# A decode step on one core: K0 and V6 loaded in two parts, V7 in four, q and gate/up as loops over padded x, and the last output rows behind the block's barrier

## The chip, the cores and the metric

The kernel runs on one core of a Trainium2 chip. The metric is device time in microseconds, as the median over runs. A profiled execution gives the trace: busy time of each engine, waits, and DMA packets. PE is TensorE, DVE VectorE, ACT ScalarE, POOL GpSimd; SP issues the transfers.

## What is computed

One decode step of attention beside a small feed-forward block, mixed by a gate. x is one row of 512; the K and V caches hold 8 groups of 32768 rows of 128 numbers in bf16, that is 8 MB per group for K and as much for V. Four query heads share each group.

```python
x = A_x
g = sigmoid((x * gate_w).sum(-1))
q = (x @ wq)                      # 32 heads of 128
p = softmax(q @ k.T * 128 ** -0.5)
a = (p @ v).reshape(1, 4096) @ wo # wo: 4096 x 512
b = (silu(x @ w_gate) * (x @ w_up)) @ w_down   # 1792 wide
out = g * a + (1 - g) * b         # 512 numbers
```

## The kernel before

**Memory.** `page` holds three pages of 8 MB (64 KB per partition). Pages 0 and 1 take the K blocks in turn, page 2 the V blocks. At first page 2 holds wq and the gate and up weights; at the end page 0 holds w_down and wo.

**The order of the transfers** is SP's program (L330 to L359): wq, x and gate_w, gate, up, K0, K1, V0, K2, V1, K3, and so on. `load_k(j)` (L312) waits until DVE has transposed the block that used the page before (`sem_tr`); `load_v(j)` (L323) waits until PE has used the whole V block before (`sem_v_done`, raised after every 8 matmuls), V0 until PE has finished gate and up (`sem_pe_h`). K7 comes in two halves. After V6 come w_down (L342), the first piece of wo (`load_wo(0)`, two of 32 columns), the five parts of V7 (`V7_CUTS`, each as soon as the V6 rows in its place are used), and the other five pieces of wo (`WO_CUTS`). Last, SP waits for the result row and stores it (L358). All of it runs through SP's one queue, in this order.

**q, gate and up.** PE turns x into a column `xT` (L369), and multiplies it with wq in 32 matmuls (L384): the weights are one column of x, and the result goes to one of four strips of 32 PSUM partitions, so that four neighbouring matmuls use different strips of the array. DVE brings q into `qblk` and `qcur` (L609 to L629), with four small matmuls of PE between (L397). Then 32 matmuls do gate and up in the same manner (L409), and ACT and DVE make the hidden vector t (L538, L632 to L646).

**The groups.** For each group DVE transposes the K block in 64 units (L687); PE multiplies each unit with the group's query (`emit_s`, L431); DVE takes the maximum (L696), POOL spreads it over the partitions (L294), ACT exponentiates (L552) and rearranges the weights into `ET` (L565). PE multiplies them with V one group later (`emit_v`, 64 matmuls, L455), after the scores of the group behind; then ACT copies the sum, PE transposes it (`emit_reduce`) and DVE picks out the four heads (L675). PE and DVE run this as loops (`hinted`, L212) with a branch for each kind of turn and a hint that says early where the loop's last branch will go.

**The end.** PE multiplies t with w_down (`emit_wd`) while V7 lands. After V7 DVE makes the attention vector `O2` and PE multiplies it with wo piece by piece: the first 24 columns into `ps_w` (`emit_wide`, L500), which DVE copies to `part` (L733); the next four into `ps_c` by `emit_rows` (L230): two matmuls of 256 columns for each column of wo, the first with 32 weight columns of which only the last is not zero (`O2z`), the second with one, so that the two halves of the row come to lie on partitions 31 and 32. Then PE turns its loop once more, and in the `Else` branch (L525) `part` is summed over its four strips (`selz` as weights, fp32) and the last two pieces of wo are added. DVE casts two rows (L745) and SP stores them. The block ends with a barrier of all engines (L253): every engine drains and signals, POOL releases them. Behind it SP waits for the store.

Of the kernel before, what the change touches and what calls it, by code (L numbers as in the profile page):

```python
# [14 lines left out]
def bass_gated_mix__gqa_block_cached__swiglu_ffn__decode_kernel(  # L15
# [23 lines left out]
    KC = D // 128  # L39
# [19 lines left out]
    WO_CUTS = [0, 2, 16, 24, 28, 30, 32]  # L59
    KW = 3  # L60
    KL = 4
# [4 lines left out]
    OW = NOUT // RPS  # L66
# [15 lines left out]
    V7_CUTS = [0, 32, 96, 160, 224, 256]  # L82

    with ExitStack() as es:
# [7 lines left out]
        sem_k = [S_(f"s_k{i}") for i in range(K_PAGES)]  # L92
        sem_k7 = S_("s_k7")
        sem_v = S_("s_v")
# [17 lines left out]
        sem_pe_sum = S_("s_pe_sum")  # L112
        sem_dve_x = S_("s_dve_x")
# [35 lines left out]
        res_row = T("res_row", [64, OW], BF16)  # L149
# [21 lines left out]
        q_row = slot[:, 0 : 2 * RQ * DH]  # L171
        q_blk = slot[:, 2 * RQ * DH : 4 * RQ * DH]
        sg = acc[:, 0:FS]
        t_row = slot[:, 0:FS]
        t_blk = slot[:, D : D + FS]
# [54 lines left out]
        def emit_rows(pe, lhs, rhs, last):  # L230
            for e in range(RPS):
                ins = pe.matmul(  # L232
                    ps_c[32 * e : 32 * e + (1 if e else SW), 0:OW],
                    lhs(e),
                    rhs[:, e * OW : (e + 1) * OW],
                    start=False,
                    stop=last,
                    skip_group_check=True,
                )
            return ins  # L240

        def emit_wo(pe, k):
# [8 lines left out]
            return ins  # L251

        with nc.Block("main") as block:  # L253
# [50 lines left out]
            def _(sp):  # L304
# [8 lines left out]
                def load_k(j):  # L313
# [36 lines left out]
                load_wo(0)  # L350
# [7 lines left out]
                sp.dma_start(  # L358
                    out[0, 0, :].rearrange("(e c) -> e c", e=RPS), res_row[SW - 1 : SW + 1, :]  # L359
                ).then_inc(sem_out, 16)  # L360

            @block.tensor
            def _(pe):
                def emit_q():
# [12 lines left out]
                    pe.wait_ge(sem_dve_prod, 1)  # L377
                    pe.wait_ge(sem_q, 16)
                    pe.wait_ge(sem_psw, 1)
                    for c in range(KC):  # L380
                        for b in range(2):
                            for s in range(NSTRIP):
                                g = 2 * s + b
                                ins = pe.matmul(  # L384
                                    ps_sc[32 * s : 32 * s + 1, b * 512 : (b + 1) * 512],
                                    xT[:, c : c + 1],
                                    wq_v[:, c, g * 512 : (g + 1) * 512],
                                    start=(c == 0),
                                    stop=(c == KC - 1),
                                    skip_group_check=True,  # L390
                                )
                    ins.then_inc(sem_pe_q, 1)
# [12 lines left out]
                    for w, (sem, base) in enumerate(((sem_fg, S_G0), (sem_fu, S_U0))):  # L405
                        pe.wait_ge(sem, 16)
                        for c in range(KC):
                            for s in range(NSTRIP):
                                ins = pe.matmul(  # L409
                                    ps_sc[32 * s : 32 * s + 1, base : base + FS],  # L410
                                    xT[:, c : c + 1],
                                    wgu[:, w, c, s * FS : (s + 1) * FS],
                                    start=(c == 0),
                                    stop=(c == KC - 1),
                                    skip_group_check=True,
                                )
                    ins.then_inc(sem_pe_h, 1)
# [27 lines left out]
                def emit_v(p):  # L445
                    part_at = pe.compute_val(((p + 7) >> 4) * 16 + 1)
                    pe.wait_ge(sem_v, p * 16)
# [42 lines left out]
                def emit_wide():  # L490
# [19 lines left out]
                    emit_wo(pe, KW).then_inc(sem_late, 1)  # L510

                emit_q()
                with hinted(pe, "groups", 1, G + 4) as (p, arm):
# [11 lines left out]
                    with pe.Else():  # L525
                        pe.wait_ge(sem_dve_w, 1)
                        emit_rows(pe, lambda e: selz[:, SW - 1 : SW] if e else selz[:, :], part, False)
                        for k in range(KL, len(sem_wo)):
                            ins = emit_wo(pe, k)
                        ins.then_inc(sem_pe_sum, 1)  # L530

            @block.scalar
            def _(act):
# [3 lines left out]
                act.wait_ge(sem_pe_h, 1)  # L537
# [39 lines left out]
            def _(dve):  # L577
# [6 lines left out]

                dve.memset(ps_sc[:, :], 0.0).then_inc(sem_psw, 1)
# [4 lines left out]
                for sem in sem_v7[1:] + [sem_k7, sem_acc]:  # L590
# [7 lines left out]
                dve.tensor_copy(xT[:, :], xg[:, 0, :]).then_inc(sem_dve_x, 1)  # L598
                dve.wait_ge(sem_dve_x, 1)
# [7 lines left out]
                dve.wait_ge(sem_pe_q, 1)  # L607
# [168 lines left out]
```

## Time and profile before

| | |
|---|---|
| median of 3 runs | 351.38 us (351.13 to 351.65) |
| the profiled execution | 352.33 us, its span 350.8 us |
| busy: PE, DVE, ACT | 174.7, 190.8, 92.9 us |
| moved by DMA | 148.14 MB, 422 GB/s over the span |
| weight-load and matmul records on PE | 2723 and 2723 |

A line of a group names the source line, engine and operation, then output and inputs, the number of instructions and their time. "DMA to landing" is the time from a transfer's issue to the last of its sixteen signals, each from one DMA engine. Issue time plus this is the moment at which the block can be used. The chain of waits lists start, length and what ran. A timeline row has in brackets how long its engine was idle before, and what ended that.

### The profile page before, as it was taken

What the parts mean: (1) busy time and instruction counts of PE and PEld (TensorE: products, weight loads), DVE (VectorE), ACT (ScalarE), POOL (GpSimd) and SP (SyncE); (2) the same over time, 40 slices, a digit from 0 to 9 for tenths busy, and PEclk for the clock granted to TensorE, in tenths of its full rate; (3) what the DMA queues carried; (4) which work ended last, traced back from release to release, by engine and by line L of the source; (5) the groups of instructions that cost most, each with busy time, mean ns of one, the idle gap of its engine ahead of it and who ended that gap; (6) DMA issues with size and microseconds to landing.
All of it is one profiled execution on the core that took longest, in us unless ns stands there. A gap on an engine that the chain in (4) does not pass through costs nothing.

```text
span 350.8 us, 7554 instructions
## 1 busy us (share of the span) xinstructions
PE 174.7 (50%) x2723; PEld 106.3 (30%) x2723; DVE 190.8 (54%) x309; ACT 92.9 (26%) x220; POOL 8.3 (2%) x29
## 2 busy tenths in 40 slices
PE   0430155455745570556435571557145585547546
PEld 0110144344234420443124321443034334422112
DVE  3060299899169801995069802993089729930001
ACT  1020000470480057003530057003800056036100
POOL 4000000000000000000000000000000000010000
PEclk9999999999975567555655566555855565559955
DMA  8998998999989999999899899998998999989994
GB/s 336 412 508 359 478 478 359 478 433 404 478 359 463 441 411 456 396 463 456 381 471 456 389 456 419 441 456 381 471 456 389 407 430 478 456 349 420 430 420 169
DMA packets 4475, 148.14 MB, mean 422 GB/s; under 512 B 501, under 2 KB 505, under 8 KB 1017
## 3 DMA queue, kind: packets, MB, share of 16 engines
q1 hardware_dynamic: 4472, 148.12, 98.3%
q8 instruction: 1, 0.02, 0.0%
q14 instruction: 2, 0.01, 0.0%
HBM read 148.11 MB, written 0.00 MB: 422 GB/s over the span
## 4 chain that ended last, share of the span: by engine, by line
DMA 63%; PE 15%; DVE 14%; issue 7%; SPq 1%; DVEq 0%
DMA page<-in_A_k_cache_dram 48%; DVE slot L687 13%; DMA page<-in_A_v_cache_dram 8%; DMA page<-in_A_wo_dram 7%; PE ps_sc L431 7%; PE ps_o L455 7%; PE ps_c L232 1%; SPq L306 0%; SPq L348 0%; SPq L334 0%; DVE oT L675 0%; DVEq L683 0%; DVE res_row L745 0%; DVEq L666 0%; SPq L330 0%
## 5 line engine op out<-in xcount | busy, mean ns | idle before, releaser
L687 DVE STREAM_TRANSPOSE slot<-page 128x512 f32<-128x512 f32 x256 | 167.0, 690 | 101.0 <-DMA page<-in_A_k_cache_dram 89.3
L431 PE MATMUL ps_sc<-qcur,slot 128*128 128x16 bf16 x2048 | 103.5, 179 | 126.9 <-DVE slot L687 113.4
L431 PEld LDWEIGHTS ps_sc<-qcur,slot 128*128 128x128 bf16 x2048 | 80.9, 107 | 151.0 <-issue 150.1
L455 PE MATMUL ps_o<-page,ET 128*16 128x512 bf16 x512 | 46.8, 541 | 21.0 <-issue 12.3
L565 ACT ACTIVATE ET<-E 32x256 bf16<-32x256 bf16 x128 | 52.8, 412 | 1.4
L547 ACT ACTIVATE nbias<-gmax 128x4 f32<-128x4 f32 x8 | 1.6, 206 | 185.7 <-POOL gmax L294 185.7
L455 PEld LDWEIGHTS ps_o<-page,ET 128*16 128x16 bf16 x512 | 16.1, 117 | 48.2 <-issue 34.5
L552 ACT ACTIVATE E<-ps_sc,nbias 128x256 bf16 x32 | 21.8, 851 | 1.7 <-ACT nbias L547 1.7
L696 DVE TENSOR_REDUCE pmax<-ps_sc 128x4 f32<-128x1024 f32 x8 | 9.8, 1225 | 4.7 <-PE ps_sc L431 4.7
L719 DVE TENSOR_REDUCE oT<-ps_o 128x4 f32<-128x64 f32 x1 | 0.2, 224 | 20.5 <-PE ps_o L469 20.5
L561 ACT ACTIVATE acc<-ps_o 128x512 f32<-128x512 f32 x8 | 4.8, 606 | 22.0 <-PE ps_o L455 22.0
L547 ACT ACT_TABLE_LOAD x8 | 10.3, 1283 | 0.1
L294 POOL PARTITION_ALL_REDUCE gmax<-pmax x8 | 3.0, 372 | 293.5 <-DVE pmax L696 293.5
L552 ACT ACTIVATION_READ_ACCUMULATOR E<-ps_sc,nbias x32 | 9.2, 287 | 0.0
L469 PE MATMUL ps_o<-ident_f,acc 128*128 128x128 f32 x32 | 5.7, 305 | 5.6 <-ACT acc L561 4.9
L369 PE MATMUL ps_m<-eye,E 2*128 2x2 bf16 x4 | 0.3, 164 | 13.3 <-DMA E<-in_gate_w_dram 13.3
L469 PEld LDWEIGHTS ps_o<-ident_f,acc 128*128 128x128 f32 x32 | 3.6, 150 | 10.1 <-ACT acc L561 8.4
L481 PE MATMUL ps_w<-page,vec 128*1 x14 | 5.3, 376 | 2.2 <-issue 0.9
L711 DVE TENSOR_REDUCE oT<-ps_o 128x4 f32<-128x64 f32 x1 | 0.2, 224 | 8.9 <-PE ps_o L469 8.9
L598 DVE CAST xT<-ps_m 128x4 bf16<-128x4 f32 x1 | 0.2, 163 | 8.9 <-PE ps_m L369 8.9
L369 PEld LDWEIGHTS ps_m<-eye,E 2*128 2x128 bf16 x4 | 0.2, 108 | 13.2 <-issue 13.2
L574 ACT ACTIVATE acc<-ps_o 128x512 f32<-128x512 f32 x1 | 0.6, 597 | 13.4 <-PE ps_o L455 13.4
(63 smaller groups left out, 44.7 us busy)
## 6 DMA issues: line engine op xcount, KB each, us to landing
page<-in_A_k_cache_dram SPq DMA_DIRECT2D x2, 4096.0 KB, 41.8
page<-in_A_v_cache_dram SPq DMA_DIRECT2D x3, 2048.0 KB, 13.5
page<-in_A_wq_dram SPq DMA_DIRECT2D x1, 4096.0 KB, 12.3
page<-in_A_v_cache_dram SPq DMA_DIRECT2D x2, 1024.0 KB, 13.0
page<-in_B_w_gate_dram SPq DMA_DIRECT2D x1, 1792.0 KB, 15.5
page<-in_B_w_up_dram SPq DMA_DIRECT2D x1, 1792.0 KB, 19.3
page<-in_B_w_down_dram SPq DMA_DIRECT2D x1, 1792.0 KB, 30.7
page<-in_A_wo_dram SPq DMA_DIRECT2D x1, 1792.0 KB, 23.5
```

Of the source, the lines that this page charges most:

```text
L232: ins = pe.matmul(ps_c[32 * e : 32 * e + (1 if e else SW), 0:OW], lhs(e), rhs[:, e * OW : (e + 1) * OW], start=False, stop=last, skip_grou ...
L294: pool.partition_all_reduce(gmax[:, :], pmax[:, :], 128, ReduceOp.max).then_inc(sem_gmax, 1)
L431: ins = pe.matmul(ps_sc[:, bass.ds(c0 + u * (SLOTS * RPU * NS) + (s * RPU + r) * NS, NS),], sv[:, s, r, e // 2, e % 2, :], qcur[:, e, :], ...
L455: ins = pe.matmul(ps_o[32 * c : 32 * c + VW, :], ET[:, k * VW : (k + 1) * VW], rows(V_PAGE, n, n + RQ), start=(k < NSTRIP), stop=(k >= NT ...
L469: ins = pe.transpose(ps_o[:, q * 128 : (q + 1) * 128], acc[:, q * 128 : (q + 1) * 128], ident_f[:, :],)
L481: pe.matmul(ps_w[0:1, :], vec[:, bass.ds(n, 1)], page[:, bass.ds(n * NOUT + o0, NOUT)], start=False, stop=False, skip_group_check=True,)
L547: act.activation(nbias[:, :], gmax[:, :], ACT.Copy, scale=-SCALE).then_inc(sem_nbias, 1)
L552: act.activation(ev[:, h, :, :], scv[:, h, :, :], ACT.Exp, bias=nbias[:, h : h + 1], scale=SCALE, accum_out=esum[:, bass.ds(j * HPG + h, 1 ...
L561: act.activation(acc[:, :], ps_o[:, :], ACT.Copy).then_inc(sem_acc, 1)
L565: ins = act.activation(etv[QP * i : QP * (i + 1), :, g, :], E[QP * g : QP * (g + 1), i * w : (i + 1) * w].rearrange("p (f m) -> p f m", f=KH),
L687: dve.transpose(slot_f[:, s * (SLOT // 2) : (s + 1) * (SLOT // 2)].rearrange("p (x g b) -> p g x b", g=NQ, b=QP), kp[:, f, :, tu * UW : (t ...
L696: dve.tensor_reduce(pmax[:, :], ps_sc[:, p * RB * NS : (p + 1) * RB * NS].rearrange("p (x h) -> p h x", h=HPG), AX.X, ALU.max,).then_inc(s ...
```

## The change

- K0 is loaded in two halves, like K7; DVE waits for the second (`sem_k0`) in the middle of the group.
- V6 is loaded in two parts, rows 0 to 160 and 160 to 256 (`V6_CUT`, `sem_v6`); V7 in four instead of five, the first with 128 of the 256 rows. All seven pieces of wo follow V7; before there were six, the first ahead of V7.
- q and gate/up become two loops of four turns with eight matmuls each. The weights are 128 columns out of `xz`, which is zero but for x in one column, shifted so that the result falls on the strip wanted. The other strips get zero added; so all matmuls accumulate onto the zeroed `ps_sc`. DVE zeroes `xz` (in `slot`) first and copies x into it; `q_row` and `t_row` move to `E`. Gate and up now stand ahead of the small matmuls for q, and `sem_pe_q` and `sem_pe_h` count the turns.
- `emit_rows` uses four strips with 128 output columns each instead of two with 256. `part` is added inside `emit_wide`, between the first and the second piece of wo that go to `ps_c`.
- The last two pieces of wo, the cast (now 128 x 128) and the store stand behind the block's barrier; the store is split between SP's and ACT's queues.

```diff
-    WO_CUTS = [0, 2, 16, 24, 28, 30, 32]
+    WO_CUTS = [0, 8, 16, 20, 24, 28, 30, 32]
-    KL = 4
+    KL = 5
+    OC = NOUT // 128
+    XW = 96 + 128
-    V7_CUTS = [0, 32, 96, 160, 224, 256]
+    V7_CUTS = [0, 128, 192, 224, 256]
+    V6_CUT = 160
...
-            for e in range(RPS):
+            for oc in range(OC):
+                e = oc % RPS
                 ins = pe.matmul(
-                    ps_c[32 * e : 32 * e + (1 if e else SW), 0:OW],
+                    ps_c[32 * oc : 32 * oc + (1 if e else SW), 0:128],
                     lhs(e),
-                    rhs[:, e * OW : (e + 1) * OW],
+                    rhs[:, oc * 128 : (oc + 1) * 128],
...
+        def store(eng, k):
+            n = RPS * 128
+            eng.dma_start(
+                out[0, 0, n * k : n * (k + 1)].rearrange("(c n) -> c n", c=RPS),
+                res_row[64 * k + SW - 1 : 64 * k + SW + 1, :],
+            ).then_inc(sem_out, 16)
...
-                    if j < G - 1:
+                    late = {0: sem_k0, G - 1: sem_k7}.get(j)
+                    if late is None:
                         cache(A_k_cache, j, p).then_inc(sem_k[p], 16)
                     else:
                         cache(A_k_cache, j, p, 0, NT // KH).then_inc(sem_k[p], 16)
-                        cache(A_k_cache, j, p, NT // KH, NT).then_inc(sem_k7, 16)
+                        cache(A_k_cache, j, p, NT // KH, NT).then_inc(late, 16)
...
-                        sp.wait_ge(sem_pe_h, 1)
-                    cache(A_v_cache, j, V_PAGE).then_inc(sem_v, 16)
+                        sp.wait_ge(sem_pe_h, KC)
+                    if j < G - 2:
+                        cache(A_v_cache, j, V_PAGE).then_inc(sem_v, 16)
+                    else:
+                        cache(A_v_cache, j, V_PAGE, 0, V6_CUT).then_inc(sem_v, 16)
+                        cache(A_v_cache, j, V_PAGE, V6_CUT, NT).then_inc(sem_v6, 16)
...
-                load_wo(0)
                 for k, sem in enumerate(sem_v7):
                     a, b = V7_CUTS[k], V7_CUTS[k + 1]
                     sp.wait_ge(sem_v_done, VTURN * (G - 1) + b // (RQ * VB))
                     cache(A_v_cache, G - 1, V_PAGE, a, b).then_inc(sem, 16)
-                for k in range(1, len(sem_wo)):
+                for k in range(len(sem_wo)):
                     load_wo(k)
-                sp.wait_ge(sem_dve_row, 1)
-                sp.dma_start(
-                    out[0, 0, :].rearrange("(e c) -> e c", e=RPS), res_row[SW - 1 : SW + 1, :]
-                ).then_inc(sem_out, 16)
...
+                    def strips(c, base, n, width, at, ps):
+                        x = [pe.compute_val(c * XW + (96 - 32 * s)) for s in range(NSTRIP)]
+                        w = [pe.compute_val(c * n + (base + at(i))) for i in range(2 * NSTRIP)]
+                        for i in range(2 * NSTRIP):
+                            ins = pe.matmul(
+                                ps_sc[:, ps(i) * 512 : ps(i) * 512 + width],
+                                slot[:, bass.ds(x[i % NSTRIP], 128)],
+                                page[:, bass.ds(w[i], width)],
+                                start=False,
+                                stop=False,
+                                skip_group_check=True,
+                            )
+                        return ins
+
+                    with pe.Fori(0, KC, 1) as c:
+                        strips(
+                            c, w0, H * DH, 512, lambda i: (2 * (i % 4) + i // 4) * 512, lambda i: i // 4
+                        ).then_inc(sem_pe_q, 1)
+                    pe.wait_ge(sem_fg, 16)
+                    pe.wait_ge(sem_fu, 16)
+                    with pe.Fori(0, KC, 1) as c:
+                        strips(
+                            c, w1, F, FS, lambda i: (i // 4) * KC * F + (i % 4) * FS, lambda i: 2 + i // 4
+                        ).then_inc(sem_pe_h, 1)
...
+                        if n == V6_CUT:
+                            pe.wait_ge(sem_v6, late_at)
...
-                    emit_wo(pe, KW).then_inc(sem_late, 1)
+                    emit_wo(pe, KW)
+                    pe.wait_ge(sem_dve_w, 1)
+                    emit_rows(pe, lambda e: selz[:, SW - 1 : SW] if e else selz[:, :], part, False).then_inc(
+                        sem_late, 1
+                    )
+                    for k in range(KW + 1, KL):
+                        emit_wo(pe, k)
...
-                    with pe.Else():
-                        pe.wait_ge(sem_dve_w, 1)
-                        emit_rows(pe, lambda e: selz[:, SW - 1 : SW] if e else selz[:, :], part, False)
-                        for k in range(KL, len(sem_wo)):
-                            ins = emit_wo(pe, k)
-                        ins.then_inc(sem_pe_sum, 1)
...
+                dve.memset(slot[:, 0 : KC * XW], 0.0).then_inc(sem_xz, 1)
...
+                dve.wait_ge(sem_xz, 1)
+                dve.tensor_copy(xz[:, :, 96], xg[:, 0, :]).then_inc(sem_xz, 1)
...
                             if t == KHU:
+                                if p == 0:
+                                    dve.wait_ge(sem_k0, 16)
...
-                    with dve.Else():
-                        dve.wait_ge(sem_pe_sum, 1)
-                        dve.tensor_copy(res_row[:, :], ps_c[0:64, 0:OW]).then_inc(sem_dve_row, 1)
-
-        nc.sync.wait_ge(sem_out, 16)
+
+        pe, dve = nc.tensor, nc.vector
+        for k in range(KL, len(sem_wo)):
+            ins = emit_wo(pe, k)
+        ins.then_inc(sem_pe_sum, 1)
+        dve.wait_ge(sem_pe_sum, 1)
+        dve.tensor_copy(res_row[:, :], ps_c[:, 0:128]).then_inc(sem_dve_row, 1)
+        for k, eng in enumerate((nc.sync, nc.scalar)):
+            eng.wait_ge(sem_dve_row, 1)
+            store(eng, k)
+        nc.sync.wait_ge(sem_out, 32)
```

More of the change, by code (lines that the diff above doesn't have):

```diff
@@ L92, in bass_gated_mix__gqa_block_cached__swiglu_ffn__decode_kernel @@
         sem_k = [S_(f"s_k{i}") for i in range(K_PAGES)]
+        sem_k0 = S_("s_k0b")
         sem_k7 = S_("s_k7")
+        sem_v6 = S_("s_v6")
         sem_v = S_("s_v")
@@ L148, in bass_gated_mix__gqa_block_cached__swiglu_ffn__decode_kernel @@
         selz = T("selz", [128, SW], FP32)
-        res_row = T("res_row", [64, OW], BF16)
+        res_row = T("res_row", [128, 128], BF16)
         eye2 = T("eye2", [2, 2], BF16)
@@ L170, in bass_gated_mix__gqa_block_cached__swiglu_ffn__decode_kernel @@
         x2 = E[0:2, 0:D]
-        q_row = slot[:, 0 : 2 * RQ * DH]
+        xz = slot[:, 0 : KC * XW].rearrange("p (c m) -> p c m", c=KC)
+        q_row = E[:, 0 : 2 * RQ * DH]
         q_blk = slot[:, 2 * RQ * DH : 4 * RQ * DH]
         sg = acc[:, 0:FS]
-        t_row = slot[:, 0:FS]
-        t_blk = slot[:, D : D + FS]
+        t_row = E[:, 0:FS]
+        t_blk = E[:, D : D + FS]
         spread = ET[:, 0 : NSTRIP * 128].rearrange("p (s m) -> p s m", s=NSTRIP)
@@ L377, in emit_q @@
                     pe.wait_ge(sem_dve_prod, 1)
+                    pe.wait_ge(sem_xz, 2)
                     pe.wait_ge(sem_q, 16)
                     pe.wait_ge(sem_psw, 1)
[L380 to L392, printed above, removed]
+                    def strips(c, base, n, width, at, ps):
[21 more added lines that the diff above has]
+                        ).then_inc(sem_pe_h, 1)
                     pe.wait_ge(sem_const, 4)
@@ L404, in emit_q @@
                     ins.then_inc(sem_pe_qp, 1)
[L405 to L417, printed above, removed]
                 sv = slot[:, :].rearrange(
@@ L589, in _ @@
                 dve.sem_inc(sem_sc, SLOTS)
-                for sem in sem_v7[1:] + [sem_k7, sem_acc]:
+                for sem in sem_v7[1:] + [sem_v6, sem_k7, sem_acc]:
                     dve.sem_inc(sem, 1)
@@ L606, in _ @@
                 )
-                dve.wait_ge(sem_pe_q, 1)
+                dve.wait_ge(sem_pe_q, KC)
                 dchain(
```

6 lines of the change are left out of this document (4 added, 2 removed).

## The prediction

> **What bounds the kernel now.** I read the page first: the span, the DMA queue, the chain by engine.
>
> ```profile
> span 350.8 us, 7554 instructions
> ...
> q1 hardware_dynamic: 4472, 148.12, 98.3%
> ...
> DMA 63%; PE 15%; DVE 14%; issue 7%; SPq 1%; DVEq 0%
> ```
>
> The kernel moves 148 MB through one queue whose packets fill 98.3% of the span, 344.8 us. The engines matter in two ways only: by when they let SP issue the next transfer, and by what they do after the last byte. So next comes the chain of waits, and with it each issue with its time to landing, in the view by source line:
>
> ```profile
> 63.35 35.62 DMA page<-in_A_k_cache_dram
> ...
> 319.62 26.26 DMA page<-in_A_wo_dram
> ```
>
> ```profile
> L306 SPq DMA_DIRECT2D page<-in_A_v_cache_dram x1: 328/328/328, 95.7 to 95.7; - x1
> DMA to landing us min/median/max: 23.6/23.6/23.6
> ...
> L306 SPq DMA_DIRECT2D page<-in_A_k_cache_dram x1: 432/432/432, 96.1 to 96.1; - x1
> DMA to landing us min/median/max: 42.6/42.6/42.6
> ...
> L306 SPq DMA_DIRECT2D page<-in_A_v_cache_dram x1: 328/328/328, 129.7 to 129.7; - x1
> DMA to landing us min/median/max: 28.3/28.3/28.3
> ```
>
> K2, the third K block, lands at 63.35 + 35.62 = 98.97; V1 at 119.3, K3 at 138.7, V2 at 158.0. Blocks of 8 MB follow each other by 19.3 to 19.4; V1 alone needs 20.4. It was issued at 95.7, only 3.2 us before K2's landing, and **1.0 us is lost**. V2, issued 9.0 us ahead of K3's landing, loses nothing. So on the last DMA engine V1's stream begins 98.97 + 1.0 - 95.7 = 4.3 us after its issue (counted in landing times). The second place with little in hand is V7:
>
> ```profile
> L342 SPq DMA_DIRECT2D page<-in_B_w_down_dram x1: 432/432/432, 286.5 to 286.5; - x1
> DMA to landing us min/median/max: 30.7/30.7/30.7
> ...
> L348 SPq DMA_DIRECT2D page<-in_A_wo_dram x1: 432/432/432, 287.0 to 287.0; - x1
> DMA to landing us min/median/max: 30.9/30.9/30.9
> ...
> L306 SPq DMA_DIRECT2D page<-in_A_v_cache_dram x1: 328/328/328, 314.1 to 314.1; - x1
> DMA to landing us min/median/max: 6.4/6.4/6.4
> ...
> L348 SPq DMA_DIRECT2D page<-in_A_wo_dram x2: 432/432/432, 320.1 to 320.6; - x2
> DMA to landing us min/median/max: 26.4/26.5/26.6
> ```
>
> w_down lands at 317.2, the first piece of wo at 317.9, the first 1 MB of V7 (issued at 314.1) at 320.5. A megabyte takes 19.35/8 = 2.4, so 0.2 is lost here and the stream began about 4.0 after the issue. The last piece of wo lands at 320.6 + 26.6 = 347.2. From there to the end is a tail of **3.6 us**:
>
> ```profile
> 345.72 0.69 DVE L733 COPY acc<-ps_w 128x512 f32<-128x512 f32 x1 [3.63 <-PE ps_w L500]
> ...
> 346.18 0.42 PE L232 MATMUL ps_c<-page,slot 128*32 128x256 bf16 x1
> ...
> 347.20 1.06 PE L232 MATMUL ps_c<-acc,selz 128*32 128x256 f32 x4 [0.17 <-issue]
> ...
> 349.16 0.42 DVE L745 CAST res_row<-ps_c 64x256 bf16<-64x256 f32 x1 [2.75 <-PE ps_c L232]
> 349.61 0.27 SPq L358 DMA_DIRECT2D out_dram<-res_row  x1
> ```
>
> The fp32 row of `part` begins at 347.20, when all of wo has landed: it stands behind a turn of the loop. The last two pieces of wo follow it, then a cast and the store, which takes 350.8 - 349.61 = 1.2.
>
> **The change part by part.** The sum is made against the profiled execution (span 350.8, own time 352.33). That lies 0.95 above the median of 351.38; I take the difference from the one and put it on the other.
>
> *K0 in halves, with the q and gate/up loops ahead of it.* What the first transposes waited for, and what now comes late:
>
> ```profile
> L306 SPq DMA_DIRECT2D page<-in_A_k_cache_dram x2: 452/474/495, 2.8 to 3.3; - x2
> DMA to landing us min/median/max: 38.1/47.6/57.0
> ```
>
> ```profile
> 13.55 0.16 DVE L598 CAST xT<-ps_m 128x4 bf16<-128x4 f32 x1 [8.92 <-PE ps_m L369]
> ...
> 13.96 3.58 PE L384 MATMUL ps_sc<-page,xT 128*1 128x512 bf16 x32 [0.45 <-DVE prod_col L600]
> ...
> 21.96 0.18 DVE L629 COPY qcur<-qblk 128x64 bf16<-128x64 bf16 x1
> ...
> 279.62 6.51 PE L455 MATMUL ps_o<-page,ET 128*16 128x512 bf16 x64 [1.81 <-issue]
> ...
> 309.36 1.23 DVE L696 TENSOR_REDUCE pmax<-ps_sc 128x4 f32<-128x1024 f32 x1 [0.58 <-PE ps_sc L431]
> ...
> 313.00 5.19 PE L455 MATMUL ps_o<-page,ET 128*16 128x512 bf16 x64 [3.68 <-DMA page<-in_A_v_cache_dram]
> ```
>
> K0 lands at 40.9, so its first half at 31.2; K1 at 60.3. Before, four strips of PE columns ran beside each other: 3.58/8 = 0.45 us per four. A padded x fills all 128 columns, so its matmuls run one after another. No row has such a one alone: from above 0.45 each, 14.4 us for 32; from below the pace at which V6 beats V5 (the colder V5 takes 6.51/64 each, V6 saves 1.3 in its last part, which comes to about 0.22 per four), 7.0. PE starts cold and is then busy without a break, so I take 9 for q and 6.5 for gate/up: done near 29.5. The small matmuls for q now stand behind gate/up, and of the 4.4 us from the end of q (17.5) to `qcur` (22.0) most follows: transposes begin near 33 to 34. A half group lasts 11 us, so K0's second half is there in time, and group 0 is done near 56, before K1 lands. In the trace group 0 ended at 63.35 and V1 was issued 32.4 later; from 60.3 the same 32.4 give 92.7 at the latest: 6.3 us in hand instead of 3.2, more than the 4.3 needed. **-1.0** on every later landing. The zeroing of 896 columns lies in DVE's idle 8.92 us before 13.55; it costs nothing, and below 1 us without that cover.
>
> *More pieces.*
>
> ```profile
> L306 SPq DMA_DIRECT2D page<-in_A_k_cache_dram x2: 432/432/433, 246.7 to 247.2; - x2
> DMA to landing us min/median/max: 37.2/41.8/46.4
> ```
>
> The second half of K7 lands 9.7 after the first, 19.35/2: a cut costs below 0.1. K0 and V6 add two, V7 has one part fewer, wo one more, the store one: +0.2, between 0 and 0.4.
>
> *V6 in two parts, V7 in four, all of wo behind.* PE takes V6 after the scores of K7 (last maximum at 309.36). They hang on K6's landing and move with it, to 308.5. In the turn of V5 1.81 us passes until the first V matmul: 310.3, and V6's first 160 rows have long landed. V7's first piece now asks for 32 matmuls of V6: half of 6.51, plus 0.3 to drain and signal. It is issued at **313.9**, no sooner than the 314.1 of before, since PE and no longer the transfer sets it. But w_down, the last thing ahead of it, lands at 317.2 - 1.0 + 0.2 = 316.4, and the 0.7 us of wo that stood between have gone behind. With a stream that starts 4.0 to 4.3 after its issue (both cases above), V7 streams on the last engine from 318.0: a gap of 1.6 us, which **swallows the gain at V1**. What follows is what took 347.2 - 317.9 = 29.3, less the 0.2 lost in it, plus 0.7 for the moved piece: 29.8. Last landing **347.8, +0.6**. Bounds: no gap, 346.2; a stream that starts 4.6 after, 348.3.
>
> In the Trainium skill, the page "DMA: Bandwidth & Descriptors" (Specifications) gives a first-byte latency of about 0.6 us for queues issued from SP. By that V7 would flow while w_down still does and nothing would be lost; V1, which lost 1.0 with 3.2 us in hand, speaks against it.
>
> *The tail.* `part` now follows the fourth piece of wo inside one turn, without a branch; its copy (0.69) is through when that piece lands. Only 2+2 columns of wo are left behind the barrier. The piece ahead of them lands 1.3 us before the last (345.9, by the chain's 319.62 + 26.26, against 347.2, with the same 512 KB behind it); its 16 matmuls take four steps of 0.11 (half of the 0.21 of a pair of 256 columns) plus 0.3 until the last is through: done 0.5 before the last landing. DVE has left its loop by then, since it waits only for `part`'s matmuls. Then, from the last landing: wait and two steps 0.35, last one through 0.3, cast of 128 instead of 256 columns 0.3, store 1.2: 2.15 instead of 3.6, **-1.45**. The store's second half, on ACT's queue, runs beside the first; no row has one: from 0 to +0.5, I take 0.
>
> Sum: +0.6 - 1.45 = -0.85: a span of 349.95 and, on the median, 350.5 to 350.6; I say **350.6 us**.
>
> **The rivals.**
>
> *A. V7 loses nothing.* The last landing is 346.2 and the time 351.38 - 1.0 - 1.45 = 348.95. For it: most DMA engines may be served sooner than the last one. Against: both issues with under 4 us in hand lost time.
>
> *B. The code behind the barrier has to be fetched.* Slower. The loop's end in the view by source line, and the page:
>
> ```profile
> L224 PEldq COMPARE_BRANCH  x11: 81/226/232, 64.5 to 347.4; - x11
> ...
> L253 PEldq DRAIN  x1: 8/8/8, 350.3 to 350.3; - x1
> L253 PEldq EVENT_SEMAPHORE  x1: 51/51/51, 350.5 to 350.5; - x1
> ```
>
> ```profile
> q8 instruction: 1, 0.02, 0.0%
> ```
>
> PE leaves its loop at 347.4 and reaches the barrier's drain at 350.3, 2.9 later; released 0.2 after that. Before, the cast and the store hid it. Now the last matmuls stand behind: the loop is left 1.5 after the fourth piece of wo lands (345.9 to 347.4 in the trace; 345.3 now), so at 346.8, drain 349.7, release 349.9, then 0.8 + 0.3 + 1.2: a span of 352.2, +1.4, **352.8**. It decides once the wait at the loop's end exceeds 1 us. It holds only if the code behind the barrier lies outside what PE has loaded; q and gate/up have shrunk by some sixty instructions and the rows grown by as many, so the place where before ran out may not be reached. In the Trainium skill, "Runtime: NRT & Kernel Launch" (Instruction fetch mechanics) says that a taken branch out of the two loaded pages forces a fetch by DMA; the one packet on q8 would fit that.
>
> *C. Part of the 2.9 us is PE's drain,* from its last matmul (349.1, just ahead of the cast) to 350.3: 1.2. Release then comes 0.9 after the last landing, the end 1.05 later than in my sum: 351.6, no change.
>
> *D. The loops stay cold.* 32 x 0.45 and 32 x 0.39 hold PE until 41, transposes start past 45, V1 is issued near 100 and 5 us are lost instead of 1.0: about 355.6. It decides from a start past 40. Against: V6's row speeds up within some 3 us.
>
> **How the numbers follow.** Forecast 0.48 (its own range 349.9 to 351.3), A 0.15, B 0.16, C 0.14, D 0.03, others 0.04. Within 0.2% means 350.7 to 352.1, about what a measurement of this kernel can tell from no change. Faster: 0.30 of the forecast and A, 0.45. Same: 0.18 of the forecast and 0.12 of C, 0.30. Slower: B, D, the rest, 0.25. The range, 349.0 to 352.7, leaves out half of A, half of B, and D.
>
> **What would show it.** V1 landing 19.4 after K2 shows the first step right, an issue of V1 after 94.7 shows it wrong. The issue of V7's first piece (313.9) and the last landing of wo (347.8) test the gap; a first piece of 4 MB that lands 9.7 after w_down means A. From the last landing to the end 2.15; idle PE between the third-last piece and the last two with nothing left to land means B or C, told apart by whether the drain comes 2.9 after the last branch or 1.2 after the last matmul. The forecast is wrong if K7's scores end well before 308.5, or if the store on ACT's queue lands late.

## The result, and the profile after

The changed kernel takes 350.29 us in the median of 20 executions (350.06 to 352.50), the kernel before 351.74 (20 executions, 351.13 to 354.09). The ratio is 0.9955, with a 95% interval of 0.9937 to 0.9973: 0.45%, or 1.6 us, faster (1.45 by the two medians). The forecast was 350.6. Executions of either kernel spread over some microseconds, so below the landings of a profiled execution are compared first, and times by their ratios. The profiled execution of after took 350.17 us, 2.16 less than that of before; the latter lay 0.6 above its median of 20.

The page of the changed kernel, then its loads in the view by source line: V1, V7's first part, and the last two pieces of wo. The rows are rounded to 0.1 us; times with two decimals below are the signals of the same traces.

```profile
span 348.6 us, 7730 instructions
...
q1 hardware_dynamic: 4760, 148.12, 98.8%
```

```profile
L321 SPq DMA_DIRECT2D page<-in_A_v_cache_dram x1: 328/328/328, 90.5 to 90.5; - x1
DMA to landing us min/median/max: 27.7/27.7/27.7
...
L321 SPq DMA_DIRECT2D page<-in_A_v_cache_dram x1: 328/328/328, 313.3 to 313.3; - x1
DMA to landing us min/median/max: 12.7/12.7/12.7
...
L368 SPq DMA_DIRECT2D page<-in_A_wo_dram x2: 3328/4678/6028, 319.2 to 325.3; - x2
DMA to landing us min/median/max: 20.7/23.4/26.2
```

V1 lands at 90.54 + 27.72 = 118.26, 19.35 after K2 (98.91): the 1.0 us is no longer lost. V7's first part lands at 326.02, 9.79 after w_down (316.23), where half a block streams in 9.71: no gap. The last piece of wo lands at 325.31 + 20.72 = 346.03; before it was 347.14. So of the 2.2 us between the two spans 1.1 lie ahead of the last landing. The other 1.0 lie behind it, in a tail of 348.6 - 346.03 = 2.57 us. The loop's end and the barrier by source line (the last branches of PE and of DVE, POOL's release, the drains), then the tail in the timeline:

```profile
L231 PEldq COMPARE_BRANCH  x11: 81/226/226, 59.2 to 345.8; - x11
L231 DVEq COMPARE_BRANCH  x6: 63/75/85, 83.8 to 345.9; - x6
```

```profile
L268 POOLq EVENT_SEMAPHORE  x2: 17/17/17, 346.1 to 346.2; - x2
...
L268 PEldq DRAIN  x1: 8/8/8, 346.0 to 346.0; - x1
L268 DVEq DRAIN  x1: 17/17/17, 346.0 to 346.0; - x1
```

```profile
346.29 0.10 PEld L240 LDWEIGHTS ps_c<-page,slot 128*32 128x32 bf16 x1 [1.18 <-DMA page<-in_A_wo_dram]
346.32 0.27 PE L240 MATMUL ps_c<-page,slot 128*32 128x128 bf16 x1 [0.94 <-PEq L268]
...
346.62 0.31 PE L240 MATMUL ps_c<-page,slot 128*32 128x128 bf16 x1
346.98 0.29 DVE L772 CAST res_row<-ps_c 128x128 bf16<-128x128 f32 x1 [3.43 <-PE ps_c L240]
347.29 0.27 SPq L263 DMA_DIRECT2D out_dram<-res_row  x1
347.30 0.60 ACTq L263 DMA_DIRECT2D out_dram<-res_row  x1
```

PE drains right behind its last branch; there is no wait of 2.9 us as before. But POOL releases the barrier (its second event) only at 346.2, 0.13 after the last landing, so the sixteen matmuls of both last pieces follow it, though the first of the two had landed at 345.39. The first matmul's idle time says so: what released it is PEq L268, the barrier, and not a DMA. (The weight load ahead of it names the DMA of its piece, which had landed 0.9 us before.)

### The profile page after: what moved, and what is told of

It is laid out like the page before. It is cut to its first block, busy times and chain, and to the rows that moved or that the text cites. A ratio compares the mean times of both kernels' runs of the same rounds, so it can differ in the third digit from the quotient of the medians.

```text
span 348.6 us, 7730 instructions
## 1 busy us (share of the span) xinstructions
PE 183.3 (53%) x2755; PEld 111.3 (32%) x2755; DVE 191.1 (55%) x311; ACT 92.8 (27%) x220; POOL 8.3 (2%) x29
## 5 line engine op out<-in xcount | busy, mean ns | idle before, releaser
L401 PE MATMUL ps_sc<-page,slot 128*128 x64 | 16.1, 421 | 1.0 <-DVE prod_col L621 1.0
L401 PEld LDWEIGHTS ps_sc<-page,slot 128*128 x64 | 7.0, 109 | 9.7 <-issue 4.8
L630 DVE CAST E<-ps_sc 128x1024 bf16<-128x1024 f32 x1 | 1.2, 1224 | 10.4 <-PE ps_sc L401 10.4
```

The source lines that it names most:

```text
L401: ins = pe.matmul(ps_sc[:, ps(i) * 512 : ps(i) * 512 + width], slot[:, bass.ds(x[i % NSTRIP], 128)], page[:, bass.ds(w[i], width)], start= ...
```

## The experiments

Each transfer ends with sixteen signals, one from each DMA engine. "Lead" is the time from a transfer's issue to the first signal of the transfer ahead of it; "lost" is what lies between the landings of the two, beyond the streaming time of the second (19.35 us for 8 MB), for the median engine and for the last one. Ratios are to the kernel before, run in the same round on the same chip. There were five rounds: that of the result; one with the four runs of the section on V1; one with `a_v7_224`, `a_q_unrolled`, `a_kl4` and `a_one_store`; one with `a_rows_inside`, `a_kl4_nolate` and `a_kl4_nolate_v7_64`; one with `a_v7_64`. The kernel before lay between 351.74 and 353.14 in their medians, so ratios of different rounds can differ by 0.4% for that alone: kernels of different rounds are compared by their traces and by their times.

### V1

`before_again` is the kernel before, unchanged.

> The kernel before, unchanged, for a second trace. If the loss of 1.0 us at V1 is a property of the kernel, V1 lands 20.4 us after K2 again, the last piece of wo near 347.2 and the span is 350.5 to 350.8. If the loss belonged to that one execution, V1 lands 19.4 after K2 and the last landing is near 346.2, with a span of 349.8. The ratio is 1.000 by either.

`b_k0_halves` is the kernel before with only this:

```diff
-                    if j < G - 1:
+                    late = {0: sem_k0, G - 1: sem_k7}.get(j)
+                    if late is None:
...
                             if t == KHU:
+                                if p == 0:
+                                    dve.wait_ge(sem_k0, 16)
```

> The kernel before with K0 loaded in halves and nothing else changed (q, gate and up stay unrolled on four strips). Theory (V1 lost time because it was issued only 3.2 us ahead of K2's landing): transposes start near 31, V1 is issued by 92, lands 19.4 after K2, the last landing is 346.2, the tail stays 3.6, the span is 349.8 and the time falls by 1.0 us (ratio 0.997). Rival (the loss belongs to the one execution): same landing times, but a ratio of 0.999 to 1.000. Rival (the loops are needed for it): transposes start past 35 and V1 still loses some tenths.

`a_k0_whole` takes the same lines out of the changed kernel.

> The changed kernel with K0 in one piece again. Theory: V1 is issued near 95.7 as before, lands 20.4 after K2, the last landing moves from 346.0 to 347.0, the span is 349.6, +1.0 us on the changed kernel (ratio to before 0.998 to 0.999). Rival (V1's loss belongs to the one execution): V1 lands 19.4 after K2 and the ratio stays 0.9955.

`a_k0_whole_v1_parts` adds a cut of V1 to it:

```diff
+                    if j == 1:
+                        cache(A_v_cache, j, V_PAGE, 0, NT // 2).then_inc(sem_v, 16)
+                        cache(A_v_cache, j, V_PAGE, NT // 2, NT).then_inc(sem_v1, 16)
```

> As a_k0_whole, with V1 loaded in two parts of 128 rows (32 KB per partition, as V7's first piece in the changed kernel) issued one right behind the other. Why V7's first piece lost nothing with 2.9 us in hand while V1 lost 1.0 with 3.2 is open. If it is the size of a partition's piece (64 KB against 32): V1 ends 19.4 after K2 though issued at 95.7, the last landing is 346.1, ratio 0.9955. If only the lead counts: 20.4 after K2, last landing 347.0, ratio 0.998 to 0.999.

| kernel | V1 issued | lead | lost, median / last | last wo | ratio (95%) |
|---|---|---|---|---|---|
| before | 95.7 | 2.7 | 0.29 / 1.06 | 347.14 | |
| before_again | 95.5 | 3.0 | 0.08 / 0.81 | 346.90 | 0.9991 (0.9965 to 1.0017) |
| a_k0_whole | 95.7 | 2.8 | 0.43 / 0.79 | 348.02 | 0.9994 (0.9971 to 1.0018) |
| a_k0_whole_v1_parts | 96.7 | 1.6 | 0.27 / 2.43 (first part) | 349.06 | 0.9994 (0.9967 to 1.0021) |
| b_k0_halves | 91.4 | 7.1 | 0.0 / 0.0 | 346.54 | 0.9969 (0.9949 to 0.9988) |
| after | 90.5 | 8.0 | 0.0 / 0.0 | 346.03 | 0.9955 (0.9937 to 0.9973) |

V1 in `b_k0_halves`, by source line:

```profile
L307 SPq DMA_DIRECT2D page<-in_A_v_cache_dram x1: 328/328/328, 91.4 to 91.4; - x1
DMA to landing us min/median/max: 27.2/27.2/27.2
```

91.43 + 27.15 = 118.58, which is 19.35 after K2's 99.23. The halves alone take the loss away; the loops aren't needed for it. With K0 whole it is back. So the theory holds, and the loss belongs to the kernel and not to one execution alone, but its size doesn't: the median engine loses 0.1 to 0.4, the last 0.8 to 1.1. Whether smaller rows help stays open: V1 in parts was also issued 1.0 later, with a lead of 1.6 instead of 2.8, and its last engine lost 2.4. Two expectations missed in the size. `b_k0_halves` has a span of 350.4 instead of 349.8, since the last engine lost 0.47 at V7 and the tail took 3.9; its profiled execution was the longest of its 12. `a_k0_whole` landed 1.0 later than expected, at 348.02, since V7 lost another 0.86 (next section). What K0's halves do is seen in the spread as well: 20 of the 35 executions of before in that round lie above the longest of `b_k0_halves` (352.21). The fastest of the two are alike, 351.03 and 350.98, so the fastest executions of before seem to lose nothing at V1; that is not traced.

### V7

`a_v7_224` cuts V7 into two parts, so that the first is issued later:

```diff
-    V7_CUTS = [0, 128, 192, 224, 256]
+    V7_CUTS = [0, 224, 256]
```

> The changed kernel with V7 in two parts, of 224 and 32 rows, so that V7 is first issued after 56 instead of 32 matmuls of V6: near 315.2 instead of 313.3, 0.6 us before w_down's first landing (315.8) instead of 2.5. Theory (a transfer streams 1.7 to 2.4 us after its issue, as in a_k0_whole_v1_parts, where V7 was issued with nothing left to move): on the last engine 1.2 us are lost, the first part of 7 MB lands 18.1 after w_down instead of 16.9, the last piece of wo at 347.2, time +1.2 us (ratio 0.999). Rival (the prediction's 4.0 to 4.3 us): 3.0 to 3.3 us are lost, last landing 349.1 to 349.4, ratio 1.005.

`a_v7_64` has `V7_CUTS = [0, 64, 192, 224, 256]`.

> The changed kernel with V7's parts cut at 64, 192, 224 and nothing else. Of the changed kernel's 20 executions, 8 lay more than 0.5 us above the fastest (350.83 to 352.50). Theory (at V7 one or two engines start late in such executions, since the issue comes only 2.5 to 3 us ahead): with the issue near 311.8, 4 us ahead, the fastest times stay at 350.1 and at most 2 of 12 lie more than 0.5 us above the fastest; median 350.2, ratio 0.995. Rival (the slow executions come from elsewhere): 4 or 5 of 12 lie over it, median 350.3 to 350.5.

| kernel | V7 issued | lead | lost, median / last |
|---|---|---|---|
| a_k0_whole_v1_parts | 317.0 | -0.6 | 2.57 / 0.31 (an engine that was 2 us late) |
| a_k0_whole | 314.6 | 1.4 | 0.48 / 0.86 |
| a_v7_224 | 314.4 | 1.5 | 0.46 / 0.95 |
| a_q_unrolled (below) | 314.3 | 1.6 | 0.42 / 0.03 (an engine that was 1.4 us late) |
| a_rows_inside (below) | 313.5 | 2.3 | 0.0 / 1.27 |
| before_again | 314.1 | 2.3 | 0.05 / 0.01 (an engine that was 1.2 us late) |
| a_one_store (below) | 313.5 | 2.4 | 0.0 / 0.49 |
| before | 314.1 | 2.5 | 0.0 / 0.15 (an engine that was 1.1 us late) |
| after | 313.3 | 2.5 | 0.0 / 0.08 |
| a_kl4_nolate (below) | 312.9 | 2.9 | 0.0 / 0.0 |
| b_k0_halves | 313.3 | 3.2 | 0.0 / 0.47 |
| a_kl4 (below) | 312.5 | 3.4 | 0.0 / 0.0 |
| a_v7_64 | 312.1 | 3.7 | 0.0 / 0.0 |
| a_kl4_nolate_v7_64 (below) | 311.6 | 4.2 | 0.0 / 0.0 |

The first row is the clearest: there V7 was issued when fourteen engines had nothing left. Its DMA share in the table of stretches (the next to last column; shares are counted where a packet starts):

```profile
314.00:316.00 2.00, 2.00 (x24) 0.73 (x20) 0.00 (x0) 2.00 (x8) 0.00 (x0) 0.50 0.98 416
316.00:317.00 1.00, 1.00 (x16) 0.37 (x12) 0.00 (x0) 0.09 (x2) 0.76 (x2) 0.50 0.14 57
317.00:318.00 1.00, 1.00 (x16) 0.40 (x12) 0.00 (x0) 0.00 (x0) 0.20 (x1) 0.61 0.28 94
318.00:319.00 1.00, 1.00 (x24) 0.32 (x16) 0.00 (x0) 0.00 (x0) 0.00 (x0) 1.00 1.53 473
```

```profile
L322 SPq DMA_DIRECT2D page<-in_A_v_cache_dram x1: 328/328/328, 317.0 to 317.0; - x1
DMA to landing us min/median/max: 12.1/12.1/12.1
```

The part of 4 MB landed 11.46 to 12.07 after its issue on the sixteen engines; less 9.71 for streaming, that is a start **1.75 to 2.36 us after the issue**, in landing times, on all of them. `a_v7_224` was issued at 314.38, sooner than I expected (315.2). With some 16.94 for the streaming of 7 MB (seven eighths of a block's 19.35) its engines started 1.9 to 2.9 after it, 2.2 in the median. Its last landing was 346.77, not the 349 of the prediction's 4.0 to 4.3, and its ratio 0.9961 (0.9935 to 0.9988). So 4.0 to 4.3 is no property of a transfer but of a late engine: `a_rows_inside`, with a lead of 2.3, has one engine that started 4.3 after the issue while the others lost nothing. `after` has none in its profile; 8 of its 20 executions lie over 0.5 us above its fastest. With the cut at 64 and 1.2 us more lead 6 of 6 lie between 350.04 and 350.21 (ratio 0.9927, 0.9904 to 0.9950): the fastest time is the same, the late ones are gone. That fits the theory. Six executions alone could be luck (if 40% are late, all six are in time once in 21), but the second kernel with this cut (last section) adds 6 of 6. Why single engines start late stays open.

### Code behind the barrier

`a_q_unrolled` puts the 64 matmuls of q, gate and up of the kernel before in the place of both loops:

```diff
-                    with pe.Fori(0, KC, 1) as c:
-                        strips(
...
+                    for c in range(KC):
+                        for b in range(2):
+                            for s in range(NSTRIP):
```

> The changed kernel with q, gate and up unrolled on four strips again, as before; the two last pieces of wo stay behind the barrier, but some 70 instructions of PE's program stand ahead of them, so that they lie past the place where the kernel before stood for 2.9 us. Theory (the stall belongs to a place in the program, which the loops keep out of reach): PE's drain comes 2.9 us after its last branch, near 348.8, the last matmuls follow it, the span is 351.2 (+2.6) and the ratio 1.003. Rival (code behind a barrier is never fetched late here): drain within 0.1 us of the last branch, span 348.6, ratio 0.9955. q, gate and up are done some 6 us sooner by either, which K0's first half, landing at 31.1, hides.

`a_rows_inside` takes the last two pieces of wo, the cast and the stores back into the block; of PE and DVE:

```diff
+                    with pe.Else():
+                        for k in range(KL, len(sem_wo)):
+                            ins = emit_wo(pe, k)
+                        ins.then_inc(sem_pe_sum, 1)
...
+                    with dve.Else():
+                        dve.wait_ge(sem_pe_sum, 1)
+                        dve.tensor_copy(res_row[:, :], ps_c[:, 0:128]).then_inc(sem_dve_row, 1)
```

> The changed kernel with the last two pieces of wo, the cast and both stores inside the block, in the last turn of the loops, as the kernel before had them (four strips and two stores stay). If the loop's last turn costs what it cost before (1.5 us from the fourth-last... piece's landing to the next matmul), the matmuls start near 346.2, as behind the barrier, the cast ends at 347.3 and the stores at 348.6; what then counts is the barrier behind it. Theory (no stall here, since PE's program is no longer than in the changed kernel): span 348.6 to 348.8, so the move behind the barrier was worth nothing by itself. Rival B of the prediction (the drain stalls for 2.9 us when PE jumps out of its loop to code that isn't loaded): drain near 349.8, span 350.1 or more.

PE's last branch and drain, first of `a_rows_inside`, then the page and the same rows of `a_q_unrolled`:

```profile
L231 PEldq COMPARE_BRANCH  x11: 82/226/232, 59.4 to 347.6; - x11
```

```profile
L268 PEldq DRAIN  x1: 8/8/8, 351.0 to 351.0; - x1
```

```profile
span 350.2 us, 7631 instructions
...
q8 instruction: 2, 0.03, 0.0%
```

```profile
L231 PEldq COMPARE_BRANCH  x11: 76/221/226, 56.5 to 347.3; - x11
```

```profile
L268 PEldq DRAIN  x1: 8/8/8, 347.5 to 347.5; - x1
```

`a_rows_inside`: 347.6 to 351.0, **3.3 us from the branch to the drain**, and a 16 KB instruction packet that starts at 348.10 and takes 1.4 within them. The stores were issued at 348.4 and would have ended at 349.7 (1.3 as in after); the barrier makes the span 351.2. Its median is 351.66, ratio 0.9964 (0.9945 to 0.9982); `a_kl4_nolate`, of the same round, has 349.92. So rival B's stall is real, and it isn't the jump out of the loop by itself, since after makes the same jump and drains at once. The packet is no sign of a stall by itself either, since every run has one such packet behind PE's last branch:

| kernel | last matmul ahead of the drain ends | last branch ends | packet | drain | drain less packet's end |
|---|---|---|---|---|---|
| before | 349.12 | 347.44 | 347.86 to 348.84 | 350.31 | 1.47 |
| before_again | 348.87 | 347.20 | 347.63 to 348.85 | 350.31 | 1.46 |
| b_k0_halves | 348.51 | 346.90 | 347.78 to 348.71 | 350.18 | 1.47 |
| a_rows_inside | 348.05 | 347.69 | 348.10 to 349.50 | 350.96 | 1.45 |
| after | 345.38 | 345.92 | 346.65 to 347.58 | 345.98 | ahead of it |
| a_q_unrolled | 346.92 | 347.42 | 347.92 to 349.07 | 347.48 | ahead of it |

Where PE stalls, the drain comes 1.45 to 1.47 after the end of the packet, though the last matmul ended 1.2 to 2.9 before the drain: it is the packet that PE waits for, and neither its matmuls nor the drain itself. In all the other runs the drain comes 0.06 after the branch, ahead of the packet. What decides between the two is argued: in `a_rows_inside` sixteen matmuls more stand ahead of the drain than in after. In `a_q_unrolled` it lies farther back still, and doesn't stall, but there a packet had come in the middle of the run. In the Trainium skill, the page "Runtime: NRT & Kernel Launch" (Instruction fetch mechanics) says that code is loaded in blocks of 16 KiB and that a taken branch out of the loaded two has to wait for a fetch; the packet's size and place agree, but no run here counts what is loaded.

`a_q_unrolled` missed both ways: no stall at the drain, yet 0.9980 (0.9958 to 1.0003) instead of 0.9955, and 351.01 at best where the changed kernel has 350.06. Its second packet on q8 says why: it starts at 27.2, in the middle of the loads, and takes 1.0. Of K0's first part, which streams then, fifteen engines land as always (median 31.00) and one 1.4 late (32.78); this engine stays behind to the end, and the last landing is 347.48. The late engine is not named in the trace, so that the packet held it up is argued from the time and the size alone. The kernel before has q unrolled as well, and no packet in the middle of its run.

### The tail

`a_kl4` has `KL = 4`, so the fifth piece of wo stands behind the barrier too.

> The changed kernel with the fifth piece of wo behind the barrier too, so that PE leaves its loop after the fourth. Theory (the barrier was released at 346.2, 0.2 us after the last landing, and the sixteen matmuls of both last pieces ran behind it): released before 345.2, only the eight matmuls of the last piece follow the last landing, cast 0.4 us sooner, span 348.2, ratio 0.9945. Rival (the store sets the end): the cast moves but the span stays, ratio 0.9955.

`a_kl4_nolate` takes DVE's wait away as well:

```diff
-                    dve.wait_ge(sem_late, 1)
```

> As a_kl4, and DVE no longer waits for the matmuls of the last row of part before it leaves its loop. In a_kl4 PE drained at 344.8, but DVE, which leaves 1.35 us after those matmuls, drained at 346.03, the same as in the changed kernel, and 24 matmuls instead of 16 stood behind the release. Theory (DVE's way out of the loop holds the barrier): DVE drains near 344.7, the barrier is released near 345.0, only the last piece's eight matmuls follow the last landing, the cast starts at 346.6 instead of 346.98, span 348.2, ratio 0.9945. Rival (what stands behind the barrier has to be fetched; a 16 KB instruction packet ran from 345.35 to 346.44 in a_kl4): the matmuls start after that packet, near 346.5, the cast at 347.3 and the span is 348.9.

`a_one_store` leaves out the output's second half:

```diff
-        for k, eng in enumerate((nc.sync, nc.scalar)):
+        for k, eng in enumerate((nc.sync,)):
```

> The changed kernel without the store on ACT's queue: the output's second half is left out, the first half is stored by SP as before. Theory (the store on ACT, 601 ns in the queue against 272 on SP, ends last): from the store's issue to the end 1.1 us as with the one store of the kernel before, span 348.4, -0.2, ratio 0.995. Rival (hidden beside SP's): span 348.6, no change; or, if it costs the whole difference of the tail to the prediction, -0.4.

DVE's first branch behind its wait for `part`'s matmuls in `a_kl4`, then the barrier, by source line:

```profile
L764 DVEq COMPARE_BRANCH  x1: 75/75/75, 344.7 to 344.7; - x1
```

```profile
L268 POOLq EVENT_SEMAPHORE  x2: 17/17/17, 346.1 to 346.2; - x2
...
L268 PEldq DRAIN  x1: 8/8/8, 344.8 to 344.8; - x1
L268 DVEq DRAIN  x1: 17/17/17, 346.0 to 346.0; - x1
```

PE was there 1.1 us sooner than in after; DVE was not, and the release stayed at 346.2. DVE goes on at 344.68, when `part`'s matmuls are through, and needs 1.35 us for its branches. So 32 matmuls instead of sixteen (the next expectation says 24, wrongly) stood behind the release, the cast came at 347.41 and the span was 349.1: a tail **0.4 longer** than in after, with the same last landing, against my expectation (ratio 0.9978, 0.9951 to 1.0004).

```profile
347.41 0.29 DVE L772 CAST res_row<-ps_c 128x128 bf16<-128x128 f32 x1 [3.87 <-PE ps_c L240]
```

Without the wait DVE drains at 344.1:

```profile
L268 POOLq EVENT_SEMAPHORE  x2: 17/17/17, 345.0 to 345.1; - x2
...
L268 DVEq DRAIN  x1: 17/17/17, 344.1 to 344.1; - x1
L268 PEldq DRAIN  x1: 8/8/8, 345.0 to 345.0; - x1
```

Now only the last piece follows its landing, and landing to cast takes 0.50 instead of 0.95 (346.35 to 346.85):

```profile
346.85 0.29 DVE L769 CAST res_row<-ps_c 128x128 bf16<-128x128 f32 x1 [3.15 <-PE ps_c L240]
```

The span is 348.5 with a landing 0.3 later than in after, the ratio 0.9920 (0.9892 to 0.9948). A fetch didn't hold the matmuls up: those of the last piece began at 346.39, while the packet ran from 345.40 to 346.67.

`a_one_store`, its span and its store:

```profile
span 349.1 us, 7729 instructions
```

```profile
L263 SPq DMA_DIRECT2D out_dram<-res_row x1: 272/272/272, 348.0 to 348.0; - x1
```

From the issue (347.95) to the end (349.09) 1.14; with ACT's store 1.32 (347.29 to 348.61). The second store costs 0.18, as the theory said. The span itself is longer, mostly for the late engine at V7 (0.49); the ratio is 0.9947 (0.9926 to 0.9967).

### A version that beats both

`a_kl4_nolate_v7_64` joins the cut at 64 with the tail of `a_kl4_nolate`.

> As a_kl4_nolate, with V7's parts cut at 64, 192, 224 instead of 128, 192, 224, so that its first part is issued near 312.0, 1.3 us sooner and 3.9 us before w_down's first landing. Theory (most engines stream 1.7 to 2.4 us after the issue, single ones up to 4.6): last landing 346.0 as in the best executions, no engine loses over 0.1 at V7, and fewer executions lie over the fastest by 0.5 us than the 8 of 20 of the changed kernel; span 348.2, ratio 0.994. Rival (the late engines have nothing to do with the lead): same span, but as many slow executions as before.

```profile
346.25 0.29 PE L240 MATMUL ps_c<-page,slot 128*32 128x128 bf16 x1
...
346.70 0.29 DVE L769 CAST res_row<-ps_c 128x128 bf16<-128x128 f32 x1 [3.02 <-PE ps_c L240]
347.02 0.27 SPq L263 DMA_DIRECT2D out_dram<-res_row  x1
```

The last landing is 346.20, the cast 0.50 behind it, the span 348.3. All 6 executions lie between 349.58 and 349.98, below the fastest of the changed kernel (350.06); the ratio is 0.9911 (0.9884 to 0.9938). The changed kernel itself was not run in this round, but the kernel before was no faster there (351.45 at best, against 351.13 beside the changed kernel). Of `a_kl4_nolate`, with V7 cut at 128, 2 of 6 lie over 0.5 above its fastest, here none.

## Why the prediction was right, and where it was wrong

- **V1: right, -1.0 on the last engine of that trace.** Issued at 90.5 (at the latest 92.7 was said), it landed 19.35 after K2, and `b_k0_halves` shows the cause. The median engine had lost only 0.29.
- **The loops: right, a little short.** The matmuls and the first transpose of the changed kernel:

```profile
L401 PE MATMUL ps_sc<-page,slot x64: 352/366/634, 14.5 to 30.2; 128*128 x64
```

```profile
L710 DVE STREAM_TRANSPOSE slot<-page x2: 671/691/711, 35.9 to 36.5; 128x512 f32<-128x512 f32 x2
```

q took 10.0 instead of 9, gate and up were done at 30.6 instead of 29.5, and transposes began at 35.9 instead of 33 to 34, since t is made ahead of them. K2 was issued at 58.0 instead of 56. Nothing came of it, with 8 us of lead at V1. Rival D fell (and its 355.6 left out the -1.45 of the tail). What I had not seen is that this kernel with unrolled code would have a packet of code in the stream and, it seems, lose 1.4 by it.

- **More pieces: right, +0.2.** By their landings parts lose 0.08 more than before at K0, 0.07 at V6, 0.17 at wo, and some 0.1 less at V7.
- **V7's gap: wrong, and the step that failed.** The issue came at 313.3 (313.9 said), since K7's last maximum came at 307.8 instead of 308.5; with a start 4.0 to 4.3 later that would still have left a gap of over 1 us. "With a stream that starts 4.0 to 4.3 after its issue (both cases above), V7 streams on the last engine from 318.0: a gap of 1.6 us": there was none, and the last landing was 346.03 instead of 347.8. This is rival A. The two cases had been read off the *last* landing, so they gave the start of the latest of sixteen engines, by chance, and I took it for the start of every transfer. At V7 of the kernel before that engine had hardly waited at all: it was 1.1 late ever since V1 and still busy with what came ahead, while the median engine went on without a gap. Where engines had nothing else to do, the runs show 1.7 to 2.4 (up to 2.9 in `a_v7_224`). The page "DMA: Bandwidth & Descriptors" (Specifications) of the Trainium skill, with its 0.6 us to the first byte, was nearer: in `a_k0_whole_v1_parts` V7's first packet started at 317.99, 0.64 after the end of its issue. But 0.6 is not the lead that a transfer needs: with a lead of 1.5 the median engine of `a_v7_224` lost 0.46. The same page (Anatomy of one DMA) has a fixed cost of about 2 us in all, for transfers issued from GpSimd; the 1.7 to 2.4 here, issued from SP, lie around it.
- **The tail: right in kind, short by 0.42** (2.57 instead of 2.15). "DVE has left its loop by then, since it waits only for `part`'s matmuls" left out the 1.35 us of its branches, and the sum left out PE's own, 0.6 from its last matmul to the drain. So both reached the barrier only at 346.0, its release came after the last landing, and the matmuls took 0.95 to the cast instead of 0.65. The store took 1.32 instead of 1.2; ACT's half costs 0.18, where I had 0. In the joined version, with both repaired but the store, the tail is 348.3 - 346.20 = 2.1.
- **Rivals B and C.** B's stall exists (3.3 us in `a_rows_inside`) but the changed program doesn't reach it. C fell: the drain follows the branch within 0.1 us, 0.6 after the last matmul, and where it comes late it comes a fixed 1.45 to 1.47 after a packet of code.
- **The sum.** Two errors went against each other: 1.8 us too much up to the last landing, 0.42 too little in the tail. By the spans the change brought 2.2, not 0.85. That 350.6 still came so near 350.29 is luck besides. The profiled execution of before was 0.6 above its median of 20, so part of the 2.2 was the luck of that execution; and the 351.38 that I subtracted from, a median of three, was 0.36 below the median of 20. By the medians of 20 the change brought 1.45, where I forecast 0.8: the forecast had the right direction and little more than half the size.

## What to carry to other kernels

A transfer's landing is that of the latest of its sixteen engines: look at all sixteen before a late landing is taken for a fixed cost, and give the issue some 3.5 us of lead where a queue must not run dry (here engines lost time at leads up to 3.2, and none from 3.4 on). What stands behind a barrier starts with the slowest engine's way out of its loop, so an engine with nothing to do should be let go early. And where a loop is left near the end of a program, look whether the drain follows the last branch at once: sixteen matmuls in between went with a stall of over 3 us.

## What else the runs showed of the hardware

- A 16 KB fetch of code beside the loads (27.2 to 28.2 in `a_q_unrolled`) goes with 1.4 us lost on one DMA engine, for good: its landings stay behind to the end.
- SP's issue of a piece of wo took up to 6.03 us (the row of L368 above) against a median of 0.47, while nine transfers ahead of it had not landed. It cost nothing here.
- A store's issue takes 601 ns on ACT and 272 on SP.
- A fetch that PE waits for costs more than its packet: PE went on 1.45 to 1.47 us after the packet's end, in four traces.
